# Attention and a gated mixer in one kernel: the same 3437 parts in another written-out order, with other PSUM banks

## The chip, the cores and the metric

One core of a Trainium2 chip runs the whole program. The metric is the device time of one execution in microseconds (us). Its engines are TensorE (PE; weight loads are shown apart as PEld), VectorE (DVE), ScalarE (ACT), GpSimd (POOL) and SyncE (SP), which here only issues DMAs. Every engine works through its own instructions strictly in program order and waits on semaphores for what other engines make.

## The reference

The inputs are q, k and v of shape (8, 8, 576, 64): batch, heads, sequence, head width. The output is (8, 576, 512).

```python
scores = scale * np.matmul(q, k.transpose(0, 1, 3, 2))
scores = np.where(block_i >= block_j, scores, -1e9)      # blocks of 64 positions
attn = softmax(scores); attn_out = np.matmul(attn, v)
x = attn_out, heads side by side                         # (8, 576, 512)
theta = x @ w_theta
y = w_tok_r @ (x * cos(theta)) + w_tok_i @ (x * sin(theta))
u = x + y
out = u + np.maximum(u @ w_ch, 0)
```

## The kernel before

Every float32 matmul is made of three float16 matmuls: an operand is split into a high half and the rest (a "low" half), and high x high, low x high and high x low are added up in PSUM. So nearly each operand costs one scaling copy (the high half, on ACT or POOL) and one subtraction (the low half, on DVE, or on POOL for some).

The work is cut into 3437 **parts**. A part is a small function that issues between one and some fifty instructions. It has a key, for instance `("mix", b, dt, th, n)`, the keys that it needs, and the labels of the PSUM banks that it takes or leaves. The function `emit` first hands a bank (0 to 6; bank 7 is fixed) to each label from the string `BANKS`, and then issues the parts in the order of the list `ORDER`, which holds part numbers. It asserts only that a part comes after all that it needs. Nothing else sets the order: `ORDER` fixes the sequence on each engine and in SP's DMA queue, and `BANKS` fixes which part has to leave a bank before another may take it.

```python
for key in keys:
    for label in parts[key].takes:
        of_label[label] = banks[int(next(names))]
for n in ORDER:
    key = keys[n]
    assert done.issuperset(parts[key].needs), key
    parts[key].f()
```

The parts, by batch `b` (8 of them), head `n` (64) and pair of heads `p` (32):

- **Weights.** For each of 17 pieces of the three weight matrices, `("w", i, 0..6)` loads float64 bits (SP), narrows them to float32 (ACT once, DVE three times), and makes the high half (step 5, ACT L444) and the low half (step 6, DVE L447).
- **Attention.** `ld` loads, `vs` takes sizes (ACT). `qh`, `kh` (POOL) and `ql`, `kl` (DVE L525, L530) split q and k; `v1` (ACT) and `v2` (DVE) split v. `s1`, `s2`, `sd` make scores (PE L551 to L579). `m` and `mn` take row maxima (DVE L596, L601), `e` is the exponential out of PSUM (ACT L606; five for a head). `high` (ACT L617) and `low` (DVE L621) split the probabilities `p`, `turn` transposes them by DMA (SP L625), `weighted` multiplies them with v (PE L644), and `normalise` (three steps on DVE: L650, L652, L656) divides into `xn` and so frees the one bank that all heads share. The first 16 heads go in two pieces, A and B.
- **Mixer.** `xh`, `xl`, `xt` split and turn x. `theta` (PE L772, 20 parts a batch), `turns` (ACT L779), `rest` (DVE L784), `size` (ACT L790) make the angle, and `sines` (ACT L796, L798) its cosine, kept in `aa`, and its sine, kept in `rr`. `z` multiplies by x (POOL L807, 20 a batch), `zh` (ACT L816) and `zl` (POOL L821, or DVE for two of five) split the product. `mix` (PE L837, L830; 48 a batch, n = 0 to 5 in turn for each of 8 banks) is the token matmul; n = 0 to 4 need the `zl` of the same n, and the first of all needs the low halves of every token weight. `u`, `uh`, `ul` take the result out of PSUM, `c` (PE L855, 32 a batch) is the channel matmul, and `out`, `fin`, `store` finish.

TensorE has nothing of the mixer to do until the first batch's `sines` are done. From then on the mixer of one batch is laid between the attention of later ones.

Of the kernel before, what the change touches and what calls it, by code (L numbers as in the profile page):

```python
# [34 lines left out]
    24, 25, 26, 27, 28, 0, 1, 2, 3, 4, 8, 9, 5, 177, 10, 178, 11, 12, 173, 174, 185, 16, 17, 32, 33, 29, 18, 19,  # L35
    186, 187, 20, 40, 21, 34, 188, 35, 56, 41, 13, 189, 36, 37, 190, 48, 42, 136, 382, 43, 381, 384, 383, 191, 57,
    387, 49, 50, 58, 44, 59, 64, 65, 66, 60, 67, 51, 193, 179, 192, 68, 180, 52, 389, 175, 176, 194, 72, 137, 394,
    69, 388, 392, 390, 393, 414, 434, 88, 391, 53, 73, 435, 45, 89, 403, 404, 96, 195, 196, 74, 437, 97, 90, 395,
    197, 436, 75, 183, 98, 398, 80, 76, 99, 198, 415, 100, 104, 416, 413, 405, 396, 397, 399, 400, 91, 406, 184, 81,
    138, 105, 417, 112, 181, 106, 418, 424, 113, 407, 425, 107, 199, 82, 114, 139, 108, 120, 419, 77, 182, 115, 83,  # L40
    420, 116, 84, 61, 426, 92, 85, 93, 128, 442, 421, 401, 440, 443, 101, 121, 129, 444, 441, 467, 540, 408, 447,
    487, 488, 122, 448, 130, 109, 123, 131, 213, 124, 117, 449, 451, 450, 132, 144, 490, 125, 203, 133, 160, 145,
    161, 146, 445, 541, 152, 466, 153, 154, 422, 200, 162, 452, 470, 446, 214, 147, 217, 163, 453, 164, 204, 205,
    471, 468, 427, 489, 206, 472, 148, 207, 456, 208, 209, 385, 155, 469, 428, 429, 495, 386, 493, 543, 542, 409,
    520, 402, 410, 473, 500, 411, 457, 458, 459, 202, 219, 412, 140, 165, 430, 215, 438, 149, 477, 150, 218, 201,
    460, 497, 496, 423, 141, 62, 431, 454, 166, 142, 474, 478, 494, 38, 167, 479, 210, 501, 220, 480, 548, 439, 504,
    168, 481, 432, 502, 498, 433, 521, 455, 491, 503, 492, 522, 461, 519, 475, 499, 14, 482, 1837, 530, 509, 505,
    78, 506, 143, 523, 510, 156, 22, 462, 463, 553, 524, 157, 464, 158, 525, 465, 1838, 54, 151, 511, 15, 23, 476,
# [1058 lines left out]
```

## Time and profile before

| | us |
|---|---|
| median of 3 runs | 746.71 |
| lowest and highest | 745.41, 746.97 |
| the profiled execution, its own time | 744.76 |
| its span, first to last instruction | 742.8 |
| TensorE busy in it | 645.7 |
| VectorE busy in it | 598.5 |
| ScalarE busy in it | 590.7 |
| GpSimd busy in it | 269.4 |
| mean granted TensorE clock | 0.973 of full speed |

The span is what the rows below divide up. The profiled execution took 1.96 us more than its span, and the median run took 1.95 us more than the profiled execution. Busy time of TensorE counts a matmul from its start to its modelled end, so that successive matmuls overlap a little.

### The profile page before, as it was taken

The page shows a single profiled execution, that of the slowest core. Times are in us where ns is not written, and L with a number is a line of the kernel's source. Part 1 is how long each engine was busy: PE and PEld are TensorE (multiplying, and loading weights), DVE is VectorE, ACT ScalarE, POOL GpSimd, SP SyncE. Part 2 cuts the span into 40 slices and gives each one's busy share as a digit, 9 for nine tenths or more (in the row PEclk, how much of TensorE's full clock was granted, in tenths as well). Part 3 has the DMA queues.
Part 4 walks back from the last instruction along what each step waited for, and adds up shares of the span by engine and source line. Part 5 has one row for each costly group of instructions (what it writes and reads, how often), then busy time and mean ns, then how long its engine had stood idle before and what let it go on. Part 6 is the DMA issues. An engine that isn't in the chain of part 4 may idle for free.

```text
span 742.8 us, 19068 instructions
## 1 busy us (share of the span) xinstructions
PE 645.7 (87%) x7899; PEld 464.3 (63%) x7899; DVE 598.5 (81%) x1157; ACT 590.7 (80%) x900; POOL 269.4 (36%) x328
## 2 busy tenths in 40 slices
PE   0336478599999999999999999999999999999997
PEld 0125354477577757776677766777567477767775
DVE  5998999989888876988879878889888889832523
ACT  5788989989998769977898779877998898547221
POOL 2120031564154704731344502670076255322710
PEclk9999669799999999999999999999999999999999
DMA  8887989798698783868878787688689527660101
GB/s 305 292 222 190 199 140 171 184 175 140 111 228 177 130 184 91 194 139 143 205 152 165 157 177 190 150 171 170 115 206 180 120 60 136 127 141 1 49 17 64
DMA packets 263399, 114.54 MB, mean 154 GB/s; under 512 B 250896, under 2 KB 250896, under 8 KB 263312
## 3 DMA queue, kind: packets, MB, share of 16 engines
q1 hardware_dynamic: 263312, 113.33, 70.2%
q8 instruction: 61, 1.00, 0.5%
q14 instruction: 26, 0.21, 0.1%
HBM read 40.96 MB, written 9.44 MB: 68 GB/s over the span
## 4 chain that ended last, share of the span: by engine, by line
PE 45%; DVE 21%; ACT 20%; DMA 6%; issue 6%; POOL 1%; SPq 0%; ACTq 0%; DVEq 0%
PE g L837 12%; ACT t L606 7%; PE g L644 6%; PE s L837 6%; DVE m L596 5%; DVE p L621 5%; PE s L772 5%; PE g L772 5%; PE g L855 4%; ACT p L617 3%; PE s L551 3%; PE s L855 3%; ACT junk L736 2%; DMA pt<-p 2%; DMA rv<-in_v 2%
## 5 line engine op out<-in xcount | busy, mean ns | idle before, releaser
L644 PE MATMUL g<-v,pt 128*128 128x65 f16 (+1 forms) x3072 | 114.9, 199 | 30.6 <-DVE xn L656 17.3
L621 DVE SCALAR_TENSOR_TENSOR p<-t,p 128x1600 f16<-128x1600 f32 (+3 forms) x80 | 120.0, 1501 | 20.2 <-ACT p L617 20.0
L644 PEld LDWEIGHTS <-pt 128*128 128x128 f16 (+1 forms) x3072 | 108.5, 102 | 42.2 <-issue 17.0
L837 PEld LDWEIGHTS <-zh 128*128 128x128 f16 x1152 | 112.9, 98 | 31.5
L837 PE MATMUL g<-wT_h,zh 128*128 128x288 f16 x432 | 124.5, 288 | 2.4 <-ACT t L606 1.3
L837 PE MATMUL g<-wT_h,zl 128*128 128x288 f16 x432 | 124.1, 287 | 1.0 <-DVE zl L821 1.0
L837 PE MATMUL g<-wT_l,zh 128*128 128x288 f16 x432 | 124.0, 287 | 0.0
L606 ACT ACTIVATE t<-s,m,size 128x448 f32<-128x448 f32 (+2 forms) x130 | 98.8, 772 | 20.3 <-DVE m L601 13.4
L617 ACT ACTIVATE p<-t 128x1600 f16<-128x1600 f32 (+3 forms) x80 | 99.7, 1248 | 1.5
L606 ACT ACTIVATE t<-g,m,size 128x320 f32<-128x320 f32 (+2 forms) x158 | 78.2, 528 | 20.0 <-DVE m L601 10.2
L807 POOL TENSOR_TENSOR aa<-aa,xn 128x256 f32<-128x256 f32 (+1 forms) x96 | 79.7, 848 | 37.1 <-ACT aa L796 19.0
L596 DVE TENSOR_REDUCE m<-s 128x1 f32<-128x576 f32 (+2 forms) x130 | 85.2, 675 | 5.0 <-PE s L557 4.7
L772 PEld LDWEIGHTS <-xT 128*128 128x128 f16 x480 | 46.2, 98 | 56.4 <-issue 7.3
L807 POOL TENSOR_TENSOR rr<-rr,xn 128x256 f32<-128x256 f32 x64 | 54.2, 858 | 59.6 <-ACT rr L798 35.5
L521 POOL TENSOR_SCALAR kh<-rk,size 128x576 f16<-128x576 f32 x32 | 27.9, 875 | 117.7 <-PE g L557 75.7
L837 PEld LDWEIGHTS <-zl 128*128 128x128 f16 x576 | 56.5, 98 | 21.2 <-issue 5.3
L551 PEld LDWEIGHTS <-qh 64*128 64x128 f16 x896 | 36.1, 97 | 50.3 <-issue 21.7
L821 POOL TENSOR_TENSOR zl<-rr,zh 128x512 f16<-128x512 f32 x32 | 42.7, 1337 | 54.9 <-ACT zh L816 52.6
L596 DVE TENSOR_REDUCE m<-g 128x1 f32<-128x320 f32 (+2 forms) x158 | 55.7, 372 | 5.1 <-PE g L557 2.2
L855 PEld LDWEIGHTS <-wch_h 128*128 128x128 f16 x512 | 47.6, 98 | 19.7 <-issue 6.4
L772 PE MATMUL g<-wth_h,xT 128*128 128x512 f16 x176 | 53.8, 388 | 1.6 <-ACT t L606 1.6
L517 POOL TENSOR_SCALAR qh<-rq,size 128x576 f16<-128x576 f32 x32 | 30.6, 958 | 48.8 <-PE g L557 18.6
(152 smaller groups left out, 1538.7 us busy)
## 6 DMA issues: line engine op xcount, KB each, us to landing
rv<-in_v SPq DMA_DIRECT2D x16, 768.0 KB, 5.6
rk<-in_qk SPq DMA_DIRECT2D x16, 576.0 KB, 4.7
rq<-in_qk SPq DMA_DIRECT2D x16, 576.0 KB, 4.7
out<-u SPq DMA_DIRECT2D x32, 288.0 KB, 2.7
w_raw<-in_w_tok SPq DMA_DIRECT2D x9, 576.0 KB, 4.8
w_raw<-in_w_theta SPq DMA_DIRECT2D x4, 512.0 KB, 5.2
w_raw<-in_w_ch SPq DMA_DIRECT2D x4, 512.0 KB, 3.8
pt<-p SPq DMA_TRANSPOSE x80, 5.8
```

Of the source, the lines that this page charges most:

```text
L517: nc.gpsimd.tensor_scalar(out=self.qh, in0=self.raw("q"), scalar1=self.of.ups[0], scalar2=0.0, op0=ALU.mult, op1=ALU.add)
L551: nc.tensor.matmul(to[hh][:, col:col + n], lhsT=qq[rows, 64 + P * i:64 + P * i + P], rhs=kk[rows, k0:k0 + n], start=nn == 0 and col % 512 ...
L596: nc.vector.tensor_reduce(out=self.m[:, i:i + 1], in_=self.scores_of(i), axis=AX.X, op=ALU.max)
L606: nc.scalar.activation(out=t[:, to:to + n], in_=self.scores_of(i), func=AF.Exp, scale=self.pair.of.scale, bias=self.m[:, NI + i:NI + i + 1])
L617: nc.scalar.mul(hi, x, LIFT)
L621: nc.vector.scalar_tensor_tensor(out=lo, in0=x, scalar=LIFT, in1=hi, op0=ALU.mult, op1=ALU.subtract)
L644: nc.tensor.matmul(o[to, i, :], lhsT=pp, rhs=vv[:, slot, hh, :], start=first, stop=last)
L772: nc.tensor.matmul(g, lhsT=xT[:, dt, xx + i, :], rhs=ww[:, dt, :], start=dt == 0 and n == 0, stop=dt == NDT - 1 and n == 2)
L807: nc.gpsimd.tensor_tensor(out=cd, in0=cd, in1=self.xns[dt][:, i0:i0 + ni, :], op=ALU.mult)
L821: engine.tensor_tensor(out=zl, in0=cv, in1=zh, op=ALU.subtract)
L837: nc.tensor.matmul(g, lhsT=zz[:, kk, cols], rhs=ww[:, kk, ts], start=(n == 0 and kk == k0 and nn == 0), stop=False)
L855: nc.tensor.matmul(g[:, 0:HS], lhsT=ww[:, dt, e * P:(e + 1) * P], rhs=uu[:, dt, th * HS:(th + 1) * HS], start=dt == 0 and n == 0, stop=dt ...
```

## The change

The parts, their functions and the tiles stay the same, and so do the instructions of every part. `ORDER` and `BANKS` are replaced by another solution of the same planner, for which longer DMA transfers were assumed. Of 3437 parts 124 keep their place in the list; half of the others move by at most a few places (the median over all is 7, one in ten moves by 30 or more), and of 375 banks 172 differ. The core of the diff is the stretch from the first `sines` (part 1884) to the first `mix` parts of batch 0 (1932, 1925, 1926), old and new:

```diff
 ORDER = [
...
-    669, 1883, 689, 701, 670, 641, 642, 754, 159, 1855, 705, 671, 707, 755, 95, 666, 760, 1884, 672, 643, 673, 686,
-    687, 706, 644, 47, 690, 87, 712, 1898, 1886, 645, 732, 708, 242, 709, 711, 691, 1889, 1893, 713, 1894, 714, 733,
-    170, 667, 710, 692, 1885, 721, 1887, 1890, 245, 715, 765, 693, 674, 716, 722, 1901, 717, 1897, 734, 1899, 675,
-    676, 742, 723, 677, 1888, 71, 718, 1891, 1892, 731, 694, 688, 239, 735, 1932, 1895, 1925, 695, 724, 703, 1926,
...
+    623, 1883, 681, 241, 624, 642, 752, 1855, 671, 672, 635, 1884, 95, 686, 171, 754, 47, 71, 707, 689, 690, 706,
+    666, 79, 643, 673, 712, 1886, 711, 1885, 708, 760, 709, 644, 1898, 710, 1887, 687, 713, 645, 691, 1890, 721,
+    692, 1893, 1889, 693, 731, 1888, 667, 674, 714, 55, 703, 1901, 1891, 1894, 732, 735, 722, 694, 716, 723, 715,
+    1897, 724, 675, 734, 717, 1892, 676, 1932, 1925, 1895, 677, 243, 688, 695, 246, 718, 1926, 736, 1899, 1909,
...
 ]
 BANKS = (
-    "5616665011301440123460123540123650123640123540123340123650123640123540123560123640123650123650123650123640123540"
...
+    "6166114141201450123650123450123640123650123540123240123650123640123640123650123650123540123560123640123560123450"
...
 )
```

The numbers of this stretch by key, as far as they are spoken of:

| number | part |
|---|---|
| 55, 71, 79, 47, 95, 87 | `w` 6, 8, 9, 5, 11, 10, step 6: the low half of a token weight (DVE L447) |
| 643, 644, 645 | `normalise` of head 9, its three steps |
| 675, 676, 677 | `normalise` of head 10 |
| 667, 674 / 688, 695 | `weighted` 10 A, 10 B / 11 A, 11 B |
| 672, 686, 693 | `low` 10 B, 11 A, 11 B |
| 690, 691, 692, 242 | `e` 11,1; `e` 11,0; `high` 11 B; `vs` of batch 2 |
| 1885, 1886 | the two halves of `z` for n = 0 (cosine), hf 0 |
| 1898 | a half of `z` for n = 3 (sine), hf 0 |
| 1890, 1889, 1893, 1894 | halves of `z` for n = 1 and n = 2 |
| 1887, 1888 | `zh` and `zl` for n = 0, hf 0 |
| 1932, 1925 / 1926 | `mix` n = 0 of the first two banks / n = 1 of one of them |

## Rows read from the trace of the kernel before

**Rows 1.** [...]

```profile
PE 645.7 (87%) x7899; PEld 464.3 (63%) x7899; DVE 598.5 (81%) x1157; ACT 590.7 (80%) x900; POOL 269.4 (36%) x328
...
PEclk9999669799999999999999999999999999999999
```

**Rows 2.** Busy time by stage: the stretch in us from the start and its length, then for each engine the busy us and the count, the granted clock, the share of time that the DMA engines were busy, and GB/s.

```profile
0.00:25.00 25.00, 5.20 (x53) 2.64 (x54) 17.04 (x34) 14.05 (x25) 4.70 (x29) 1.00 0.87 311
25.00:150.00 125.00, 70.37 (x1007) 48.35 (x1008) 118.36 (x274) 113.53 (x189) 30.74 (x38) 0.85 0.85 193
150.00:720.00 570.00, 552.57 (x6702) 399.54 (x6700) 455.16 (x835) 459.53 (x681) 233.94 (x262) 1.00 0.69 142
720.00:743.00 23.00, 17.56 (x144) 13.80 (x141) 7.89 (x16) 3.55 (x6) 0.00 (x0) 0.94 0.17 65
```

**Rows 3.** What VectorE waited for between 25 and 150 us: us in total, how often, the longest.

```profile
DVE r L650 <- PE g L644: 3.7, 3, 1.8
DVE p L621 <- ACT p L617: 1.0, 2, 0.6
```

**Rows 4.** What TensorE waited for from 150 us to the end: us in total, how often, the longest.

```profile
PE g L644 <- DMA pt<-p: 3.4, 3, 1.5
PE s L855 <- ACT t L606: 2.3, 5, 0.9
...
PE g L837 <- DVE zl L821: 1.0, 2, 0.6
```

**Rows 5.** TensorE in order of time around 145 us: start, length, instructions merged by line (L644 `weighted`, L837 `mix`), and in brackets its idle time just before and what ended it.

```profile
138.02 1.19 PE L644 MATMUL g<-v,pt 128*128 128x65 f16 x33 [3.33 <-DVE xn L656]
141.63 0.98 PE L644 MATMUL g<-v,pt 128*128 128x65 f16 x15 [2.43 <-DVE m L596]
145.34 1.95 PE L644 MATMUL g<-v,pt 128*128 128x65 f16 x33 [2.72 <-DVE xn L656]
147.22 0.42 PE L837 MATMUL g<-wT_h,zh 128*128 128x288 f16 x1
...
149.77 0.29 PE L837 MATMUL g<-wT_l,zh 128*128 128x288 f16 x1
149.89 0.62 PE L644 MATMUL g<-v,pt 128*128 128x65 f16 x15
150.35 0.29 PE L837 MATMUL g<-wT_h,zh 128*128 128x288 f16 x1
```

**Rows 6.** ScalarE in the same stretch (L796 and L798 `sines`, L606 `e`, L617 `high`, L816 `zh`).

```profile
132.35 2.62 ACT L796 ACTIVATE aa<-aa,half_pi 128x2048 f32<-128x2048 f32 x2
134.87 1.89 ACT L798 ACTIVATE rr<-rr 128x2048 f32<-128x2048 f32 x1
...
137.43 1.28 ACT L606 ACT_TABLE_LOAD   x1
138.73 0.62 ACT L606 ACTIVATE t<-g,m,size 128x320 f32<-128x320 f32 x1
...
142.02 0.62 ACT L816 CAST zh<-aa 128x512 f16<-128x512 f32 x1
```

**Rows 7.** GpSimd (POOL) in the same stretch (L807 `z`, L821 `zl`).

```profile
136.85 1.17 POOL L807 TENSOR_TENSOR rr<-rr,xn 128x256 f32<-128x256 f32 x1 [9.56 <-ACT rr L798]
137.98 0.73 POOL L807 TENSOR_TENSOR aa<-aa,xn 128x256 f32<-128x256 f32 x1
...
142.49 1.17 POOL L807 TENSOR_TENSOR rr<-rr,xn 128x256 f32<-128x256 f32 x1
143.62 1.15 POOL L821 TENSOR_TENSOR zl<-aa,zh 128x512 f16<-128x512 f32 x1
```

**Rows 8.** VectorE in the same stretch (L784 `rest`, L447 the low half of a weight, L621 `low`, L656 the last step of `normalise`, L596 `m`).

```profile
128.71 0.73 DVE L784 SCALAR_TENSOR_TENSOR rr<-g,size,aa 128x512 f32<-128x512 f32 x1
...
134.02 0.68 DVE L621 SCALAR_TENSOR_TENSOR p<-t,p 128x512 f16<-128x512 f32 x1
...
137.48 0.48 DVE L656 TENSOR_TENSOR xn<-g,r 128x320 f32<-128x320 f32 x1
137.88 1.81 DVE L596 TENSOR_REDUCE m<-s 128x1 f32<-128x448 f32 x3
...
142.16 0.91 DVE L621 SCALAR_TENSOR_TENSOR p<-t,p 128x512 f16<-128x512 f32 x1 [0.58 <-ACT p L617]
...
145.11 0.80 DVE L447 SCALAR_TENSOR_TENSOR wT_l<-w_val,size_tok,wT_h 128x576 f16<-128x576 f32 x1
```

**Rows 9.** Groups of GpSimd instructions by line: count | busy us in all, mean ns of one | idle us just before them, and what ended it.

```profile
L821 POOL TENSOR_TENSOR zl<-rr,zh 128x512 f16<-128x512 f32 x32 | 42.7, 1337 | 54.9 <-ACT zh L816 52.6 <-PE g L644 2.3
```

**Rows 10.** TensorE around 344 us, in order of time.

```profile
342.68 0.41 PE L830 MATMUL g<-xT,w_unit 128*128 128x288 f16 x2
344.13 1.67 PE L644 MATMUL g<-v,pt 128*128 128x65 f16 x48 [1.04 <-DMA pt<-p]
```

**Rows 11.** The DMA issues that turn `p`: count, and the median us from issue to landing.

```profile
pt<-p SPq DMA_TRANSPOSE x80, 5.8
```

**Rows 12.** GpSimd near the end: the `zl` of n = 1 of the last batch, first half of the channels.

```profile
693.93 1.16 POOL L821 TENSOR_TENSOR zl<-rr,zh 128x512 f16<-128x512 f32 x1
```

**Rows 13.** TensorE when it comes to use it: the `mix` of n = 1, last batch (the first of the two matmuls at 698.69).

```profile
698.69 0.29 PE L837 MATMUL s<-wT_h,zh 128*128 128x288 f16 x1
```

More of the change, by code (lines that the diff above doesn't have):

```diff
@@ L34 @@
 ORDER = [
[177 rows of a table removed]
[178 rows of a table added]
 ]
 BANKS = (
-    "5616665011301440123460123540123650123640123540123340123650123640123540123560123640123650123650123650123640123540"
-    "1235401236401234501236501236501234601236401236401235401236401234601236401235401236501236501234560465645656656501"
-    "5415440155460464516501401312046556645510406665451060644645056505156150641650105655540156556041650464404014661015"
-    "624653326543501662634200352465331260453"
+    "6166114141201450123650123450123640123650123540123240123650123640123640123650123650123540123560123640123560123450"
+    "1236501236501236401236401234501234601234601236401236501234501235401236501236501234601236401236561465645545651406"
+    "4416144604605505465401101256146454454414056650510460655065455156405160540651016465456016466016410545551405610401"
+    "624065634153402056254316143543631056462"
 )
```

347 rows, old and new, of the table ORDER are left out of this document.

## The prediction

> **What bounds the kernel now.** I read the page first, then busy time by stage, then who waited for whom in each stage, and last the four engines in order of time where one stage passes into the next. The page shows no engine full over the whole span: TensorE is busy for 87%, VectorE for 81%, ScalarE for 80% [rows 1]. An average over the span hides two limits. Until 150 us TensorE starves: from 25 to 150 us it is busy for 70.37 of 125 us, while VectorE is busy for 118.36 and ScalarE for 113.53 [rows 2]. VectorE stands still for 6.64 us of this stretch and names hardly anything that it waited for [rows 3]. So the work of VectorE, and close behind it that of ScalarE, sets how long the start takes. From 150 to 720 us TensorE is busy for 552.57 of 570 us [rows 2]: it is the bound there, and only the other 17.43 us are there to be won. After 720 us it idles for 5.44 us more, which is mostly the way from the last matmul over VectorE and SP to the last store. A new order can therefore gain or lose at three places: the moment from which TensorE is full (the knee), the 17.43 us of holes, and the end.
>
> The holes are many and small: from 150 us on the transposes of `p` account for 3.4 us in three waits, a bank that an exponential must leave for 2.3 us in five, a `zl` of VectorE for 1.0 us in two [rows 4]. The clock is at its full level from 150 us on but for the last moments; at the knee it is at the lower one: the matmuls from 147.22 us follow each other at 0.24 us, those from 150.35 us at 0.12 us [rows 1, 5].
>
> **The change part by part.** It removes and adds no instruction, no DMA and no byte; everything is moved. I compared the two lists engine by engine.
>
> *Up to the knee.* Both orders place the same VectorE work ahead of the last `rest` of batch 0, which is the last VectorE step before `sines` (the trace's durations add up to 134.4 us old and 134.8 us new), and the same ScalarE work ahead of `sines` (120.8 us in both). With two engines that are nearly full, the same work takes the same time: 0 us. The bounds: a gain cannot pass the 6.64 us that VectorE idles [rows 2], and I allow a third of it, 2.2 us, to either side.
>
> *The knee itself.* Here the new list differs most. Old: weighted 10 A, 10 B and 11 A run with 3.33, 2.43 and 2.72 us of idle before them, then the first two `mix` parts, then weighted 11 B, and at 150.35 us TensorE reaches mix n = 1 (part 1926) and idles little from there [rows 5]. New: the first two `mix` parts stand ahead of weighted 11 A, in the hole of 2.72 us. The work ahead of part 1926 is the same in both, so its start compares them. I follow the new order from the last `rest`, at 128.71 us in the old trace.
>
> VectorE. From there to the last step of normalise 9 the old list needs 8.77 us (128.71 to 137.48) [rows 8]. The new list takes two `kl`, one weight piece and a small step out of this stretch (2.3 us) and puts in two other weight pieces (parts 71, 79: 1.5 us at a pitch of 0.75), two maxima of head 11, four of head 12 and two small steps (3.0 us; three maxima took 1.81 [rows 8]). So normalise 9 starts at 137.5 + 2.2 = 139.7 us, and weighted 10 A at 140.2 instead of 138.02. After it come a small step (0.4 + 0.15), `low` 11 B (0.8), one maximum (0.7) and the last token weight (part 55: 0.8), which ends at 142.6 us; in the old order the last one ends at 145.11 + 0.80 = 145.9 [rows 8].
>
> POOL. The old list begins `z` with a sine part, which waits until ScalarE has finished the sine at 134.87 + 1.89 = 136.8 us; the new one begins with the two halves of n = 0, cosine, which is there at 132.35 + 2.62 = 135.0 [rows 6, 7]. `zh` of n = 0 follows the first exponential after the table load, at 139.3 instead of 142.02 us, because `vs`, an exponential and `high` now come later. POOL has done two halves and four more by 139.3 (six at 0.7 us), so `zl` of n = 0 runs from 139.9 to 141.1; the old one ran from 143.62 to 144.8 [rows 7].
>
> TensorE. Weighted 10 A and 10 B end at about 142.0 us, the two `mix` may start at 142.6 with the last weight, and take 2.7 us as before (147.22 to 149.89) [rows 5]: 145.3. Normalise 10 is done by then (about 144.9), 11 A takes 1.95 us and 11 B 0.45 us: part 1926 starts at 147.7 us, 2.6 us sooner than 150.35.
>
> Against this stands a price. The weight pieces now run while POOL multiplies. The row of `low` with 512 columns shows what that does: 0.68 us at 134.02, before POOL starts, and 0.91 us at 142.16, when POOL works; POOL's own multiplications take 1.17 instead of 0.73 us at such moments [rows 7, 8]. Three weight pieces and one `low` at 0.2 to 0.3 us each cost 0.8 us. **The knee: -1.8 us.** Its bounds are -3.4 (no such price, and the clock rises earlier since TensorE no longer stops from 140 us on, which would take 0.7 us from 11 A: 33 such matmuls took 1.95 us at 145.34 and 1.19 at 138.02 [rows 5]) and +0.6 (each of these four loses all of POOL's 0.73 us: 2.4 us more).
>
> *The middle.* For every TensorE part after the knee I took the newest part of another engine that it needs, through its tile or its bank, and set the TensorE work that the list puts between the two against the duration of that part (for a turn, from the issue of its own queue to the landing). Where the work is shorter, the difference is a shortfall. This is a count of places, and no time: it adds up to 59.9 us for the old list, of which the trace shows 17.43 us as holes, and to 53.7 us for the new. The old count finds its largest values where the trace waits, such as at 344.13 us, 1.04 us for a transpose [rows 10]. By kind, transposes go from 10.2 to 8.9, banks held by exponentials from about 19 to 13, and `mix` waiting for `zl` goes the other way, from 2.2 to 9.8. In the same ratio the holes shrink by 17.43 x (1 - 53.7 / 59.9) = 1.8 us. **The middle: -1.8 us**, bounded by -6.2 (the count's whole difference) and +7.6 (the longer stand behind `zl` in full, and nothing else).
>
> That transposes hardly win has a reason that the list shows: one takes 5.8 us from issue to landing [rows 11], and the TensorE work between `low` and `weighted` is 9.9, 9.6 and 9.7 us in the old list for the three heads that waited (31, 34, 52) and 9.9, 9.8 and 10.1 in the new, while heads 20, 61 and 63 come closer (10.1 to 9.7, 11.1 to 9.0, 13.1 to 7.4).
>
> *The end.* The last parts on TensorE, VectorE and SP are the same kinds at the same distances, so the final 5.44 us stay. In the last batch the `mix` of n = 1 stands 3.4 us of listed work sooner (some 2.8 us of time), while its `zl` on POOL moves little; the old margin was 698.69 - (693.93 + 1.16) = 3.6 us [rows 12, 13], so it falls to under 1 us. **The end: +0.5 us**, between 0 and 1.2 (the listed shortfall there).
>
> **The sum.** 0 - 1.8 - 1.8 + 0.5 = -3.1 us. The profiled span of 742.8 becomes 739.7 us, its own time 744.76 becomes 741.7, and, as the median of the runs lies 1.95 us above the profiled execution, the median 746.71 becomes 743.6 us.
>
> **The rivals.** *VectorE and POOL collide at the knee, and nothing is gained.* For it: POOL's `z` starts 1.8 us sooner and the new list puts three weight pieces beside it; rows 7 and 8 show that both sides lose. If each of the four subtractions loses a whole multiplication the knee gives -1.8 + 2.4 = +0.6; with the end's +0.5 and a middle at half its gain (-0.9) the time is 746.9 us, no change. Against it: the rows show a partial loss, 0.23 us of 0.68. [...]
>
> *POOL's subtractions come too late for TensorE, and the kernel gets slower.* The place is `mix` n = 0 and 1 of batches 4, 5 and 7 and n = 2 and 4 of batches 0 and 2, where the new list leaves about 1 us too little between `zl` and `mix`. A `zl` on POOL takes 1.34 us [rows 9], and POOL is in order: one late `zh` holds the `z` behind it. If the 7.6 us of added shortfall come true by three quarters and the other savings of the middle fail, the sum is -1.8 + 5.7 + 0.5 = +4.4 us: 751.1 us. It decides for slower from a loss of 2.8 us there. Against it: of all counted shortfall the old trace shows only 0.29, and its own `zl` waits come to 1.0 us [rows 4].
>
> *It is only a reshuffle*, with gains and losses of the holes at random: that is inside the first rival's time.
>
> **How the numbers follow.** The forecast 743.6 us has 0.48. No change (746.9 us) has 0.24, because the knee's gain rests on positions that one late instruction spoils. Slower (751.1 us) has 0.28. The three runs of the kernel before spread by 1.6 us (745.41 to 746.97), so 0.2%, 1.5 us, is about what can be told from no change. The range takes the knee's lower bound with the middle's gain doubled (-3.4 - 3.6 + 0 = -7.0) on one side, and most of the slower case on the other: 739.7 to 750.5 us. Chances: faster 0.48, same 0.24, slower 0.28.
>
> **What would show it.** Right: the first POOL multiplication starts near 135 us; mix n = 0 stands ahead of weighted 11 A near 143 us, and n = 1 starts near 148 to 149; TensorE's idle time from 150 to 720 us is 14 to 17 us; VectorE still idles about 6 us between 25 and 150. Wrong: the knee comes after 150 us because the last token weight or normalise 10 is late; `zl` of POOL heads the waits of TensorE in the middle; or VectorE idles much more before 150 us because a transpose or a load of the new SP order lands late, which the sum holds at zero.

## The result, and the profile after

The changed kernel takes 751.23 us (median of 6 runs, 748.62 to 751.77) where the kernel before takes 746.38 (6 runs, 745.41 to 747.59): the ratio is 1.0059, with an interval of 1.0043 to 1.0075. It is slower by 4.9 us. The forecast was 743.6 us; 751.2 lies outside the range. The profiled execution of after takes 751.37 us with a span of 749.6, against 744.76 and 742.8 before; of these 6.8 us of span some 2 are the spread of single executions. All lines of the code stand one line further down in the file (L606 is L607, and so on): `e` is L607, `low` L622, `weighted` L645, `mix` L838, `zl` L822, and the small step `mn` that turns the maxima of a head into the bias of its exponentials is L602.

The page of after, busy time and granted clock, as [rows 1] of before. Each digit of PEclk is the clock that TensorE was granted in one of 40 slices of the span (18.7 us here, 18.6 us before), in tenths of full speed; 9 is 90% or more. In both traces the granted clock was either full or half of that: half from 138.44 to 148.68 us in after and from 139.45 to 149.69 us in before, for example.

```profile
PE 646.1 (86%) x7899; PEld 463.1 (62%) x7899; DVE 602.4 (80%) x1157; ACT 593.6 (79%) x900; POOL 267.8 (36%) x328
...
PEclk9998689799999999999999999999999999999999
```

Busy time by stage, as [rows 2] (the columns are those of rows 2):

```profile
0.00:25.00 25.00, 5.20 (x53) 2.70 (x54) 17.39 (x33) 14.45 (x28) 8.44 (x31) 1.00 0.82 296
25.00:150.00 125.00, 70.16 (x1010) 47.41 (x1010) 118.67 (x269) 112.66 (x182) 29.48 (x36) 0.86 0.84 192
150.00:720.00 570.00, 545.33 (x6636) 392.96 (x6633) 454.30 (x835) 459.60 (x680) 227.84 (x260) 1.00 0.69 143
720.00:750.00 30.00, 25.41 (x208) 20.02 (x205) 12.05 (x22) 6.85 (x13) 2.02 (x3) 0.99 0.16 60
```

The work is the same, VectorE's 3.9 us more apart. By 150 us TensorE has done as much as before. The loss is in the middle: TensorE is busy for 545.33 instead of 552.57 of 570 us, so its holes grew from 17.43 to 24.67 us, by 7.24. Compared at moments up to which TensorE has been busy for equally long, after is level with before at 150 us (0.2 us behind), 1.6 us behind at 185, 4.0 at 260, 6.6 at 415 and 7.1 at 450 us; from there on the distance stays between 6.6 and 7.4 us. (The expectations of the first runs go by a count that gives 8.5 us at 415 us.) What TensorE waited for from 150 us on, as [rows 4]:

```profile
PE s L856 <- ACT t L607: 3.6, 4, 1.4
PE s L838 <- ACT t L607: 3.0, 4, 1.2
PE g L645 <- DVE xn L657: 2.8, 5, 0.8
PE g L838 <- ACT t L607: 2.5, 4, 1.2
...
PE s L356 <- POOL diag L350: 1.2, 1, 1.2
...
PE g L645 <- DMA pt<-p: 0.6, 1, 0.6
```

The transposes, 3.4 us before, are down to 0.6: here the order did what the prediction's count promised, and more. Banks that an exponential must leave (`<- ACT t`, all rows together) went from 8.7 to 12.7 us, and the bank of `weighted`, which `normalise` must leave (`xn`), from 0.2 to 2.8. No row names a `zl` of POOL.

The knee, TensorE in order of time, as [rows 5]:

```profile
143.04 2.89 PE L645 MATMUL g<-v,pt 128*128 128x65 f16 x48 [2.30 <-DVE xn L657]
145.74 0.43 PE L838 MATMUL g<-wT_h,zh 128*128 128x288 f16 x1
...
148.60 1.81 PE L645 MATMUL g<-v,pt 128*128 128x65 f16 x48
150.25 0.28 PE L838 MATMUL g<-wT_h,zh 128*128 128x288 f16 x1
```

VectorE ahead of it, as [rows 8] (L785 `rest`, L448 the low half of a weight, L657 the last step of `normalise`):

```profile
129.91 0.74 DVE L785 SCALAR_TENSOR_TENSOR rr<-g,size,aa 128x512 f32<-128x512 f32 x1
...
135.75 2.49 DVE L448 SCALAR_TENSOR_TENSOR wT_l<-w_val,size_tok,wT_h 128x576 f16<-128x576 f32 x2
138.16 0.68 DVE L602 TENSOR_SCALAR m<-m,size 128x2 f32<-128x2 f32 x1
138.76 1.36 DVE L448 SCALAR_TENSOR_TENSOR wT_l<-w_val,size_tok,wT_h 128x576 f16<-128x576 f32 x1
...
142.51 0.48 DVE L657 TENSOR_TENSOR xn<-g,r 128x320 f32<-128x320 f32 x1
142.91 0.78 DVE L602 TENSOR_SCALAR m<-m,size 128x2 f32<-128x2 f32 x1
...
144.88 0.80 DVE L448 SCALAR_TENSOR_TENSOR wT_l<-w_val,size_tok,wT_h 128x576 f16<-128x576 f32 x1
```

The two `mix` parts stand ahead of weighted 11 A as forecast, yet part 1926 starts at 150.25 us, where it was at 150.35. POOL's first multiplication starts at 135.2 us, as forecast, and from then on VectorE's steps take longer: three weight pieces (2.49 us for two, 1.36 us for the third, at 0.81 us each alone) lose 1.5 us together, and a step of two numbers per partition, normally 0.22 us, takes 0.68 and 0.78.

### The profile page after: what moved, and what is told of

It is laid out like the page before. It is cut to its first block, busy times and chain, and to the rows that moved or that the text cites. A ratio compares the mean times of both kernels' runs of the same rounds, so it can differ in the third digit from the quotient of the medians.

```text
span 749.6 us, 19051 instructions
## 1 busy us (share of the span) xinstructions
PE 646.1 (86%) x7899; PEld 463.1 (62%) x7899; DVE 602.4 (80%) x1157; ACT 593.6 (79%) x900; POOL 267.8 (36%) x328
## 4 chain that ended last, share of the span: by engine, by line
PE 39%; DVE 33%; ACT 17%; issue 8%; DMA 1%; POOL 1%; ACTq 0%; DVEq 0%; POOLq 0%; SPq 0%
PE g L838 9%; DVE m L597 7%; DVE p L622 7%; PE s L838 6%; ACT t L607 6%; PE s L773 5%; PE g L773 5%; PE g L645 4%; ACT p L618 3%; PE g L856 3%; PE s L856 3%; DVE m L602 2%; PE s L552 2%; DVE v L538 2%; DVE xp L762 1%
## 5 line engine op out<-in xcount | busy, mean ns | idle before, releaser
L622 DVE SCALAR_TENSOR_TENSOR p<-t,p 128x1600 f16<-128x1600 f32 (+3 forms) x80 | 120.1, 1502 | 23.5 <-ACT p L618 23.2
L838 PEld LDWEIGHTS <-zh 128*128 128x128 f16 x1152 | 112.9, 98 | 32.2
L645 PE MATMUL g<-v,pt 128*128 128x65 f16 (+1 forms) x3072 | 113.5, 198 | 21.9 <-DVE xn L657 8.2
L645 PEld LDWEIGHTS <-pt 128*128 128x128 f16 (+1 forms) x3072 | 107.2, 102 | 36.1 <-issue 15.0
L838 PE MATMUL g<-wT_h,zh 128*128 128x288 f16 x432 | 124.6, 288 | 4.7 <-ACT t L607 2.5
L838 PE MATMUL g<-wT_h,zl 128*128 128x288 f16 x432 | 124.2, 287 | 0.6 <-DVE zl L822 0.6
L838 PE MATMUL g<-wT_l,zh 128*128 128x288 f16 x432 | 124.2, 287 | 0.0
L607 ACT ACTIVATE t<-s,m,size 128x448 f32<-128x448 f32 (+2 forms) x130 | 98.0, 772 | 26.2 <-DVE m L602 12.9
L808 POOL TENSOR_TENSOR aa<-aa,xn 128x256 f32<-128x256 f32 (+1 forms) x96 | 75.4, 802 | 74.6 <-ACT aa L797 49.2
L607 ACT ACTIVATE t<-g,m,size 128x320 f32<-128x320 f32 (+2 forms) x158 | 79.1, 531 | 25.0 <-DVE m L602 12.0
L597 DVE TENSOR_REDUCE m<-s 128x1 f32<-128x448 f32 (+2 forms) x130 | 85.3, 673 | 4.4 <-PE s L558 3.4
L838 PEld LDWEIGHTS <-zl 128*128 128x128 f16 x576 | 56.5, 98 | 25.2 <-issue 8.8
L808 POOL TENSOR_TENSOR rr<-rr,xn 128x256 f32<-128x256 f32 x64 | 58.1, 917 | 23.9 <-ACT rr L799 23.9
L552 PEld LDWEIGHTS <-qh 64*128 64x128 f16 x896 | 36.7, 98 | 44.0 <-issue 15.5
L822 POOL TENSOR_TENSOR zl<-rr,zh 128x512 f16<-128x512 f32 x32 | 42.9, 1346 | 51.3 <-ACT zh L817 51.2
L773 PE MATMUL g<-wth_h,xT 128*128 128x512 f16 x184 | 55.3, 382 | 2.2 <-ACT t L607 2.2
L849 DVE SCALAR_TENSOR_TENSOR ul<-u,size_ch,uh 128x576 f16<-128x576 f32 x32 | 28.0, 879 | 31.5 <-ACT uh L845 31.5
```

Of the source, the lines that this page charges most:

```text
L552: nc.tensor.matmul(to[hh][:, col:col + n], lhsT=qq[rows, 64 + P * i:64 + P * i + P], rhs=kk[rows, k0:k0 + n], start=nn == 0 and col % 512 ...
L597: nc.vector.tensor_reduce(out=self.m[:, i:i + 1], in_=self.scores_of(i), axis=AX.X, op=ALU.max)
L607: nc.scalar.activation(out=t[:, to:to + n], in_=self.scores_of(i), func=AF.Exp, scale=self.pair.of.scale, bias=self.m[:, NI + i:NI + i + 1])
L622: nc.vector.scalar_tensor_tensor(out=lo, in0=x, scalar=LIFT, in1=hi, op0=ALU.mult, op1=ALU.subtract)
L645: nc.tensor.matmul(o[to, i, :], lhsT=pp, rhs=vv[:, slot, hh, :], start=first, stop=last)
L773: nc.tensor.matmul(g, lhsT=xT[:, dt, xx + i, :], rhs=ww[:, dt, :], start=dt == 0 and n == 0, stop=dt == NDT - 1 and n == 2)
```

## The experiments

**Where in the order the loss lies.** Four lists were put together from the two. A cut is made at a TensorE part: all parts of one list up to it, then the rest in the other list's order, each with the banks of its list (in the runs with two cuts 13 and 6 of the 375 digits, in the one at part 2080 one, were changed at the seams). In short:

```diff
-    for n in ORDER:
+    first = LIST_A[:LIST_A.index(PART) + 1]
+    for n in first + [n for n in LIST_B if n not in first]:
```

Old, then new from 150 us on (PART = 695):

> The old list up to and with weighted 11 B (part 695, the last TensorE part before the knee), then all other parts in the new list's order with the new list's banks. Theory A, the new order of 150 to 415 us loses 8 us by itself, wherever it starts from: 751 us (746.4 + 4.9). Theory B, the new start leaves VectorE and ScalarE with more to do after the knee, and the middle pays for that: 746 us or less (743 to 746), since the old start comes ahead.

New up to 150 us, then old:

> The mirror image: the new list up to and with weighted 11 B, then the old list's order and banks. Theory A (the new order of 150 to 415 us loses by itself): 746 us, as before, since both traces reach the knee at the same moment (150.2 and 150.3 us). Theory B (the new start leaves work behind): 751 us or more.

Old, then new from 415 us on (PART = 1329):

> The old list up to and with the diagonal block of pair 20 (part 1329, at 415 us in the old trace), then the new list's order and banks. Theory A: 745.7 us (746.4 less the 0.7 us that the new trace wins back between 490 us and the end), within 1 us of before. If the new order loses in the middle because TensorE is let down by a state that the late part makes good again, this one would be faster still, 743 us.

New up to 415 us, then old:

> The new list up to and with the same part, then the old list's order and banks. Theory A: 752 us (746.4 + 8.5 of the new trace's lag at 415 us, less what the old late part has of slack; 751 to 755). If the late part of the old list makes the loss good: 747 us.

Measured against before: 1.0068 (1.0042 to 1.0094), 1.0028 (1.0011 to 1.0045), 1.0015 (0.9997 to 1.0033) and 1.0086 (1.0060 to 1.0111). Both lists with the new order between 150 and 415 us lose 4 to 6 us, as theory A said. Of the other two, the one with the new order from 415 us on can't be told from before. The one with the new start is 1.8 us slower, clear of noise, though its trace reaches the first `mix` of n = 1 (part 1926) at 148.6 us instead of 150.35: from 150 to 280 us TensorE then stands still for 5.4 us, where it does so for 2.8 in before. Neither theory foresaw that: A had said no change, B 751 us or more. So theory A holds in the main, and a new start in front of the old order has a price of its own, which no run explains. Two more lists take half of that stretch each from the new list, with the old one on both sides (two cuts, at parts 1000 and 1329, and at 695 and 1000).

> The old list up to and with weighted of head 24 (part 1000, at 280 us in the old trace), the new order from there up to the diagonal block of pair 20 (415 us), the old order for the rest; banks as in each stretch, 13 digits changed at the seams. If the loss is spread over the stretch from 150 to 415 us: 748 us (746 + 2 to 3). If it arises once, soon after the knee, and is only carried on: 746 us. If all of it is here: 751 us.

> The old list up to and with weighted 11 B (part 695), the new order from there up to weighted of head 24 (part 1000, 280 us), the old order for the rest; 6 digits of banks changed at the seam. With the loss spread over the stretch: 748 us (746 + 2, between 747 and 749), as the 3.7 us of the run with the new order from 280 to 415 us leave about 1 to 2. If what goes wrong before 280 us is made good by the old list behind it: 746 us.

The new order from 280 to 415 us alone gives 749.53 us, 1.0050 (1.0035 to 1.0065); from 150 to 280 us alone 747.77 us, 1.0020 (1.0004 to 1.0036). The loss is spread over the stretch: 1.7 us in its first half and 3.6 in its second add up to the 4.9 us of the whole list, within the noise.

**The banks.** Each bank dealt anew: the free one that was left longest ago, in either list. The wide scores keep banks 0 to 3. In the kernel only the digits of the string `BANKS` change (190 of 375 in the new list, 160 in the old); the rule that they follow, in short:

```diff
-    of_label[label] = banks[int(next(names))]
+    of_label[label] = banks[min(free(label), key=left_at)]
```

> The new list, but each taken bank is the free one that the list left longest ago (the first four for the wide scores stay fixed): 190 of 375 digits differ from the new ones. Theory K (the new choice of banks makes TensorE wait for exponentials): 746 to 748 us. Theories P and S (the banks are all full at those moments, by the trace the one taken was the first to come free at 11 of the 15 waits of over 0.25 us for one): 750.5 to 752 us.

> The old list with the banks dealt by the rule of the run that dealt them anew for the new list: the free one left longest ago, 160 of 375 digits differ. That run was 11 us slower than the new list with its own banks. If the rule itself is bad for this kernel (it hands the four banks of the wide scores to others, and the next pair of heads starts late): 756 us, 10 us more than before. If the rule is fine and only the new order needs just its banks: 746 to 748 us.

New list: 762.33 us, 1.0230 (1.0208 to 1.0251), 11 us slower than with its own banks. Old list: 753.66 us, 1.0095 (1.0069 to 1.0120), 8 us slower. None of the theories had foreseen the first. The second shows that the rule is bad for this kernel, whatever the list; so the first doesn't say that the new banks are the cause, nor does it clear them. Against them as the cause stands only the trace of after: at 17 of the 21 waits of over 0.25 us behind 150 us that ended when a bank was left, no other bank had come free sooner (the expectation above counts 11 of 15). That speaks against the new banks; it doesn't show that they cost nothing.

**A step of 0.2 us that waits for POOL.** The chain of waits of after runs over VectorE for 33% of the span (21% before), and one piece of it led to a cost that both lists bear. Four engines at one hole, in order of time (POOL's row merges two instructions, the second of which ends at 174.12 + 2.27 = 176.39 us):

```profile
174.12 2.27 POOL L822 TENSOR_TENSOR zl<-rr,zh 128x512 f16<-128x512 f32 x2
175.17 1.24 DVE L602 TENSOR_SCALAR m<-m,size 128x5 f32<-128x5 f32 x1
176.53 0.62 ACT L607 ACTIVATE t<-g,m,size 128x320 f32<-128x320 f32 x1 [1.41 <-DVE m L602]
178.32 0.28 PE L838 MATMUL g<-wT_h,zh 128*128 128x288 f16 x1 [1.25 <-ACT t L607]
```

VectorE multiplies five maxima by a number, and that takes 1.24 us (0.22 to 0.23 us where POOL rests): it ends at 176.41, 0.02 us behind POOL. All exponentials of the head wait for it, and TensorE for the bank that the first of them leaves. It is no single case: 27 of the 80 such steps of after take over 0.35 us, 17 of 80 in before, and every one of these ends 0.02 to 0.03 us behind the end of a POOL instruction. Their time above 0.23 us adds up to 11.7 us in after and 7.5 before; from 150 to 420 us to 5.7 and 2.6. Two neighbours on the same engine are never held in either trace: the maxima themselves (reductions that read PSUM; those over 320 columns took at most 0.49 us with POOL working and without) and the first step of `normalise`, also a multiplication or addition of 128x5, but from PSUM (0.15 to 0.17 us with POOL working and without).

So the step from SBUF to SBUF (128x5 to 128x5) is held, 1.24 us for 0.23, and the one from PSUM is not, 0.16 us. The traces don't show what makes the difference: the second step of `normalise`, a reciprocal of 128x5 from SBUF to SBUF, took at most 0.19 us with POOL working too. That a source in PSUM, or another form of source and target, would free the step was a guess, and the two tries put it to the test.

First try, with the maxima in PSUM:

```diff
+                self.most = o_bank[:, 328 + NI * (self.n % 4):328 + NI * (self.n % 4) + NI]     # NI = 5
-            nc.vector.tensor_reduce(out=self.m[:, i:i + 1], ...
+            nc.vector.tensor_reduce(out=self.most[:, i:i + 1], ...
-            nc.vector.tensor_scalar(out=self.m[:, NI + a:NI + b], in0=self.m[:, a:b], ...
+            nc.vector.tensor_scalar(out=self.m[:, NI + a:NI + b], in0=self.most[:, a:b], ...
```

> The new list and its banks; the maxima of a head are left in PSUM (free columns of the bank of weighted) instead of SBUF, so that the small step that turns them into the bias of the exponentials reads PSUM. No instruction is added or taken away. In the trace of after this step (the group m of 128x5) takes 1.2 us instead of 0.2 where a POOL instruction is running, and ends 0.02 us behind it; the step of normalise that reads PSUM in the same form takes 0.16 us with or without POOL. Theory P (POOL holds up this step, all exponentials of a head wait for it, TensorE for their banks): the step falls to about 0.2 us everywhere, TensorE's holes from 150 to 420 us fall from 16.2 us by 3 to 4, and the kernel takes 747.5 us (746.5 to 749). Theory S (the order of the queues themselves, POOL's hold is a side show): the step gets short, the time does not: 750.5 to 751.5 us.

> The same edit in the old list, with its banks. Here the step loses 2.6 us to POOL from 150 to 420 us, where the new one loses 5.7, and 3.6 us behind that. Theory P: a gain of 1.5 us (744 to 746), less than in the new list, so that the two lists come nearer by 2 us or more. Theory S: no change, and the two lists stay 4.9 us apart.

Both take 846 us, 100 us more, and answer another question than the one asked. The step itself is no longer held (215 to 223 ns on average in each of its four forms, new list), but the free columns lie in the bank of `weighted`, and VectorE's maxima and TensorE's `weighted` now wait for each other's semaphores. The step by form, then the waits, all of the new list (count | busy us, mean ns | idle before):

```profile
L603 DVE TENSOR_SCALAR m<-g,size 128x5 f32<-128x5 f32 x24 | 5.3, 223 | 11.5 <-PE g L646 10.5 <-PE g L580 0.5
```

```profile
PE g L646 <- DVE g L598: 46.7, 25, 6.1
```

```profile
DVE g L598 <- PE g L646: 37.6, 21, 4.1
```

Second try: SBUF as before, but six elements read as three rows of two and written as one row of six, so that source and target differ in form. This is for heads 16 to 63; the exponentials then take their bias from the new places (not shown).

```diff
-            nc.vector.tensor_scalar(out=self.m[:, NI + a:NI + b], in0=self.m[:, a:b], ...
+                x = self.m[:, 0:6]
+                x = bass.AP(x.tensor, x.offset, [x.ap[0], [1, 3], [2 - self.hh, 2]])
+                nc.vector.tensor_scalar(out=self.m[:, 6:12].rearrange("p (a b) -> p a b", b=2), in0=x, ...
```

> The new list and its banks. For heads 16 to 63 the small step that turns the maxima into the bias of the exponentials reads and writes SBUF as before, but takes six elements, read in three rows of two and written as one row of six (a maximum or two are written twice), so that its source and its target have different first dimensions. No wait is added, unlike in the run with the maxima in PSUM, where VectorE's maxima and TensorE's weighted came to wait for each other. Theory P (POOL holds up this step in the form of 128x5 and 128x4, and all exponentials of a head wait for it): the step takes about 0.22 us everywhere, the holes from 150 to 420 us fall from 16.2 to 12 or 13 us, the kernel takes 747.5 us (746.5 to 749). Theory S (the order of the queues themselves; POOL's hold is a side show): 750.5 to 751.5 us. If the step keeps its 1.2 us in this form, the run tells nothing.

> The same edit in the old list, with its banks. Theory P: 744.5 us (743.5 to 745.5), since the step loses less here (2.6 us from 150 to 420 us and 3.6 behind it, of which less lies on the way to a hole). Theory S: no change, 746 us.

New list: 744.18 us, 0.9974 (0.9961 to 0.9987). Old list: 741.05 us, 0.9935 (0.9914 to 0.9957). Both gain more than theory P had said, 6 to 7 us and 5 us; theory S falls. The old list with this edit beats both kernels. The step by form, in after and then in the new list with six elements:

```profile
L602 DVE TENSOR_SCALAR m<-m,size 128x5 f32<-128x5 f32 x24 | 12.7, 530 | 0.7
L602 DVE TENSOR_SCALAR m<-m,size 128x4 f32<-128x4 f32 x24 | 7.8, 324 | 0.3
```

```profile
L603 DVE TENSOR_SCALAR m<-m,size 128x6 f32<-128x6 f32 x48 | 10.3, 214 | 1.0
```

And the moment of the hole above in the new list with six elements, POOL and VectorE:

```profile
174.71 2.26 POOL L831 TENSOR_TENSOR zl<-rr,zh 128x512 f16<-128x512 f32 x2
```

```profile
175.76 0.22 DVE L603 TENSOR_SCALAR m<-m,size 128x6 f32<-128x6 f32 x1
175.89 1.76 DVE L771 TENSOR_TENSOR xp<-xn,xp 128x640 f16<-128x640 f32 x1
```

POOL is at work as before, the step takes 0.22 us, and now the next VectorE instruction is held: 1.76 us where it takes 0.81 alone (0.79 to 0.83 in the traces of before and after). At this moment VectorE is spared little, and what is won is the order: the exponentials of the head are let go first. Over the whole span it is spared more. Its busy time, 602.4 us in after and 598.5 in before, is with six elements, in the new list and then in the old:

```profile
PE 645.1 (87%) x7899; PEld 462.5 (62%) x7899; DVE 595.5 (80%) x1157; ACT 593.6 (80%) x900; POOL 270.8 (36%) x328
PE 641.1 (87%) x7899; PEld 462.1 (63%) x7899; DVE 594.1 (81%) x1157; ACT 590.3 (80%) x900; POOL 271.5 (37%) x328
```

That is 6.9 and 4.4 us less, so most of the hold is gone and not moved to the next instruction. How much of the gain comes from the shorter work and how much from the exponentials that are let go sooner wasn't separated.

TensorE from 150 to 420 us, after, then the new list with six elements, before, and the old list with six:

```profile
150.00:420.00 270.00, 253.85 (x3193) 182.12 (x3190) 229.53 (x432) 230.16 (x342) 111.71 (x126) 1.00 0.75 157
150.00:420.00 270.00, 256.95 (x3248) 184.24 (x3244) 228.57 (x435) 232.85 (x349) 112.75 (x127) 1.00 0.76 159
150.00:420.00 270.00, 260.21 (x3324) 188.56 (x3322) 231.65 (x436) 235.54 (x351) 112.94 (x132) 1.00 0.80 161
150.00:420.00 270.00, 261.03 (x3324) 189.63 (x3323) 231.32 (x439) 237.19 (x355) 114.24 (x132) 1.00 0.79 161
```

Its holes there fell from 16.2 to 13.1 us in the new list and from 9.8 to 9.0 in the old, so the new list is behind by 4.1 us of holes instead of 6.4. That is what one would see if the hold made some 2 us of the loss, since the new list has the step meet POOL's instructions more often there (5.7 us of held time against 2.6). The times agree but don't show it: 3.1 us stay between the lists of 4.9, and a difference of 1.8 us is less than the 2 us either way that the intervals of the four times leave open together. Shown is that the step in its old form costs either list some 5 us or more. That this explains part of the difference between them is likely, and the greater part of the difference has another cause.

All heads in this form, old list:

```diff
+            first, to, rows, row = {"all": (0, 6, 1, 2 - self.hh), "A": (2, 6, 1 - self.hh, self.hh), "B": (0, 12, 0, 1)}[piece]
+            x = self.m[:, first:first + 1]
+            x = bass.AP(x.tensor, x.offset, [x.ap[0], [rows, 3], [row, 2]])
+            nc.vector.tensor_scalar(out=self.m[:, to:to + 6].rearrange("p (a b) -> p a b", b=2), in0=x, ...
```

> The old list with the step of the biases in the six-element form for all 64 heads, not for heads 16 to 63 alone. Up to 150 us the step loses 1.3 us to POOL in the old list, where VectorE is the bound and idles only 6.6 of 125 us. If these 1.3 us lie on the way to the knee: 740 us (1 us less than the 741.05 us of the run for heads 16 to 63). If VectorE's idle time takes them up: 741 us. Either way faster than the kernel before by 5 us.

741.44 us, 0.9940 (0.9920 to 0.9961): no more than for heads 16 to 63. Up to the knee the hold on this step costs nothing that the end shows.

**What stays between the lists.** Five TensorE parts of the new list were moved a little later, past work that was ready.

```diff
-    ..., 2136, 275, 968, ..., 2152, 2110, ...
+    ..., 2136, 968, ..., 2152, 275, 2110, ...        # likewise 773, 794, 930 and 898
```

> The new list with the six-element step, and five TensorE parts set 1 to 3 TensorE parts later, past work that was ready: the sums of batch 3 (part 275), weighted 14 A, 15 A and 21 (773, 794, 930) and the narrow scores of pair 10 (898). In the run with the six-element step TensorE stood 1.2, 0.45, 0.97, 0.51 and 0.5 us ahead of these five. Theory M (the rest of the loss is TensorE standing ahead of parts that are listed too early): the holes of 150 to 280 us fall from 5.5 to 2 or 3 us and the time from 744.2 to 741.5 us (740.5 to 742.5). Theory N (the inputs are late because VectorE and ScalarE are behind, and what is filled here opens again at the next part): 744 us, with holes elsewhere.

744.98 us, 0.9991 (0.9977 to 1.0004), against 744.18 us without the move: nothing won. Theory M falls. TensorE's longest waits from 200 to 285 us, without the move and then with it (L356 the sums of a batch, L654 `weighted`, L552 scores; L859 `c`, L841 `mix`):

```profile
PE s L356 <- POOL diag L350: 1.2, 1, 1.2
PE g L654 <- DVE xn L666: 0.5, 1, 0.5
PE g L552 <- ACT u L851: 0.5, 1, 0.5
```

```profile
PE g L859 <- ACT u L845: 1.1, 1, 1.1
PE g L841 <- ACT t L610: 0.7, 1, 0.7
```

The holes that were filled opened again at the next part that needs VectorE or ScalarE. Next, the six-element step with a cut of the first kind, old and then new, at part 695 (150 us) and at part 2080 (200 us):

> The old list up to and with weighted 11 B (part 695), then the new list's order and banks, with the six-element step for heads 16 to 63. Theory V (from 150 to 200 us VectorE is full, and the new order asks more of it there): 743.5 to 745 us, as the new list with this step (744.2). Theory W (the loss is spread over the whole way to 415 us): also 743 to 744.5 us. If the new start is what leaves the loss: 741 us.

> The old list up to and with the theta part 2080 (200 us in the old trace), then the new list's order and banks (one digit changed at the seam), with the six-element step for heads 16 to 63. Theory V: 741 to 742 us, as the old list with this step (741.05), since the stretch that loses is the old one's. Theory W: 743 to 744 us.

744.13 us, 0.9979 (0.9966 to 0.9993), and 744.16 us, 0.9972 (0.9958 to 0.9986). The new list may have the old start, and the old order up to 200 us, and loses the same 3 us. The second time is above theory V's 741 to 742 us, so V falls; theory W fits the times. TensorE from 200 to 280 us, busy us of 80, old list, new list, and old list up to 200 us, all three with six elements:

```profile
200.00:280.00 80.00, 79.88 (x994) 1.00 0.81 181
```

```profile
200.00:280.00 80.00, 77.44 (x899) 1.00 0.76 163
```

```profile
200.00:280.00 80.00, 77.93 (x905) 1.00 0.69 145
```

Some 2 of the 3 us arise here, where the old order keeps TensorE full. Which parts of the new one do it wasn't settled. The waits from 150 to 420 us with six elements give a lead. TensorE's largest in the new list is for the bank of `weighted`, which `normalise` of the head before must leave; the old list has no such wait there. And ScalarE waits for `mn` twice as long as in the old list (the second line below, and the third for the old list), although the step is no longer held:

```profile
PE g L654 <- DVE xn L666: 2.7, 4, 1.0
ACT t L616 <- DVE m L603: 11.3, 8, 3.0
```

```profile
ACT t L615 <- DVE m L602: 5.6, 7, 2.0
```

So these two steps of VectorE come late in the new order. No run changed that alone, and its share in the 3 us is open.

**Longer transfers.** One more load of 295 KB ahead of each transpose of `p`, in both lists.

```diff
+            nc.sync.dma_start(out=spare, in_=qk[self.pair.b, 0, 0][:, 0])
             nc.sync.dma_start_transpose(out=self.turned[...], in_=...)
```

> The old list and banks (the step of the biases as it was), with one more load of 295 KB into a spare tile issued on SP's queue ahead of each of the 80 transposes of p, so that these land later; the loads feed nothing. In the trace of before, 12 weighted parts after 140 us have less than 1 us between the landing of their transpose and their start, and 21 less than 1.5; in the trace of after 9 and 14. If transposes land 1.5 us later, the missing times add up to 15.8 us in the old list and 9.9 in the new (1 us: 7.5 and 3.7). Theory D (the new order is made for longer transfers, and loses where they are short): 758 us here (753 to 764), and the new list within 2 us of it, or faster.

> The same edit in the new list. Theory D: 757 us (753 to 761), no more than 1 us above the old list with the same loads, and faster than it if the transposes land 2 us later or more. Theory E (the room that the new order gives the transposes is worth nothing even then): it stays 4 to 5 us behind the old list with the same loads.

Old list: 753.74 us, 1.0112 (1.0081 to 1.0143). New list: 762.78 us, 1.0228 (1.0204 to 1.0253), 9 us behind instead of 5. The issues of the transposes (count, median us to landing) and TensorE's waits for them after 150 us, for the old list and then for the new:

```profile
pt<-p SPq DMA_TRANSPOSE x80, 6.2
```

```profile
PE g L647 <- DMA pt<-p: 7.8, 8, 1.9
```

```profile
pt<-p SPq DMA_TRANSPOSE x80, 6.0
```

```profile
PE g L648 <- DMA pt<-p: 7.1, 7, 2.5
```

They land only 0.2 to 0.4 us later than without the loads (5.8 us in both lists, [rows 11]), so this isn't the test of 1.5 us that was meant. As far as it goes it speaks against theory D: the new list waits for transposes nearly as much as the old one, and is 9 us behind where theory D has at most 1 (and theory E 4 to 5). What the loads cost beyond these waits wasn't looked into.

## Why the prediction was wrong, step by step

*What bounds the kernel.* This held: by 150 us TensorE had done as much as before, and the time was lost in TensorE's holes behind it.

*Up to the knee, 0 us: 1.2 us were lost.* The last `rest` came at 129.91 us for 128.71, inside the bounds of 2.2. It is partly the spread of single executions: over eight kept traces with the old start it comes at 127.0 to 130.2 us (median 128.2), over five with the new one at 128.6 to 130.5 (129.2). (Runs that change something ahead of 150 us are left out.) Partly it is the order: VectorE is busy ahead of this `rest` for 117.1 to 117.4 us in the five and for 115.1 to 115.7 in the eight, where the sum had 0.4 us between the lists by fixed durations.

*The knee, -1.8 us: 1.3 us were won, and the price was sized too low.* The orders on TensorE and POOL were as told, `z` from 135.2 us. From the last `rest`, where the sum starts, to part 1926 the traces have 21.4 to 22.9 us with the old start (median 21.65) and 20.0 to 20.4 us with the new one (20.3). In the pair of before and after the later `rest` eats this gain, and 0.1 us is left. The sum had 19.0 us without the price and 19.8 with it, so the price came to 1.3 us instead of 0.8. I read a partial loss out of [rows 7, 8]: `low` took 0.91 us instead of 0.68. A full hold that begins late looks the same: POOL was at the end of an instruction (the next one starts at 142.49 us). The 9 `kl` of before that begin inside a POOL instruction bear it out: each is longer than the free 0.81 us by what is left of that instruction less some 0.2 us (correlation 0.99), and not at all where less than 0.2 us is left. So a step can lose nearly a whole instruction of POOL; `mn` lost 1.0 us (1.24 for 0.23). The three weight pieces lost 1.5 us, and two steps `mn` ahead of normalise 9, which the sum didn't price, 0.7 us more (0.68 and 0.43 us for 0.22 each); its last step came 12.6 us behind the last `rest`, where the sum had 11.0. This is the first rival's mechanism. Its reading, that a subtraction can lose a whole multiplication, was nearer to what the traces show than mine, and I had set it aside on the strength of one row. (Four full holds of 0.73 us would have been 2.1 us above the price, not the 2.4 of that bound.) Of the lower bound, the 0.7 us for weighted 11 A came: its 33 matmuls took 1.25 us instead of 1.95, since the clock was full again from 148.68 us (149.69 before). That it rises sooner because TensorE no longer stops was an estimate, and no run shows it.

*The middle, -1.8 us: failed, +7.2 us.* This is the step that made the forecast wrong: the count of shortfalls, and the ratio of 53.7 to 59.9 that turned it into time. It set each listed distance against a duration out of one trace, as if durations stayed, and it looked only at the newest part that each TensorE part needs, not at how late VectorE and ScalarE come to that part. At least one duration doesn't stay: `mn` takes 0.18 to 0.23 us where POOL rests or up to 1.24, as the order has it meet POOL or not, and it gates a whole head. By the holes of single traces that is some 2 of the 6.4 us lost from 150 to 420 us; what makes the rest isn't known. The count saw the transposes shrink, and too little (10.2 to 8.9; measured 3.4 to 0.6 us). Banks held by exponentials it saw fall from 19 to 13; they rose from 8.7 to 12.7 us. The upper bound, +7.6, was near the outcome by luck: it was taken from late `zl`, and those were not there.

*The end, +0.5 us.* From 720 us on TensorE idled for 4.2 us (749.6 - 720 - 25.41) instead of 5.2: 1 us won in this pair. (The 5.44 us of the prediction run to 743 us; the span ends at 742.8.) The `zl` of POOL wasn't late.

*The rivals.* "POOL's subtractions come too late" gave 751.1 us, and 751.2 was measured, but its mechanism was not there: waits for `zl` fell from 1.0 to 0.6 us, and none was POOL's. Its time was right by chance. POOL does cost time, by what it holds up on VectorE and not by its own lateness; how much of the loss between the lists that makes isn't shown.

*What stays open.* The greater part of the loss: 3 us between the lists stay with six elements. They are placed (two thirds between 200 and 280 us, by single traces) and not explained; the late `normalise` and `mn` are a lead. That the new banks have no part in it was argued from the trace, not shown. Why the new start costs 1.8 us in front of the old order is open too.

## What to carry to other kernels

Before moving work between queues, look for short VectorE steps whose time varies with GpSimd: a row whose mean is twice its shortest time (here 0.53 us for 0.22), on an instruction that gates another engine, can be a wait in disguise, and changing its form was worth 5 us here where reordering 3437 parts lost 5. A count of distances with fixed durations can't see such a step, and where an instruction can be held, its upper price in a sum is, by the traces here, the rest of the longest instruction that may hold it (1.0 us for `mn`). When a filled hole opens again one part later, look at the engines that feed the one that stands there. Judge a gain at one place from several traces, each counted from the same event: here that showed 1.3 us which the one pair of traces hid.

## What the runs showed of the hardware

A multiplication of 128x2 to 128x5 numbers from SBUF to SBUF took 0.18 to 0.23 us alone and up to 1.24 us when POOL was at work; where it took over 0.35 us, it ended 0.02 to 0.03 us behind POOL's instruction. Read as 3x2 and written as 6 it took 0.21 us on average over 48 of them (0.22 us at the one moment shown above, with POOL at work); what in the form makes the difference, no run shows. A hold that looks partial (0.23 us on 0.68) can be a full one that began late: over 9 `kl` the loss was the rest of POOL's instruction less 0.2 us. Columns of one PSUM bank that two engines use for different things came with waits for each other (46.7 us of TensorE's time), although no number was shared; these are waits for semaphores, which the program holds, and no run shows what the chip itself would have done.
